# Inverse softmax sums of a banded attention: one turn for two head pairs and a way through DRAM in place of six turns, and K loaded for four heads

## The chip, the cores and the metric

The kernel runs on one core of one Trainium2 chip. The core has a matrix engine (PE, with a separate path PEld that loads stationary operands), a vector engine (DVE), an activation engine (ACT), a general engine (POOL) and a queue (SP) that issues transfers between DRAM and on-chip memory, which 16 DMA engines carry. Each engine works through its own queue in order. The metric is the device time of one execution in microseconds; the figure for the kernel before is the median of 3 runs.

## The reference

Two stages. The first is an attention of 4 batches, 8 heads, 768 positions and head size 64, in which a query sees the 96 latest keys and the first 8 (global) keys; the second sends each of the 3072 resulting rows of 512 through a mixture of 8 experts whose weights are balanced by eight rounds of row and column normalisation.

```python
scores = scale * np.matmul(q, k.transpose(0, 1, 3, 2)) + bias   # bias: distance times a slope per head
scores = np.where(keep, scores, -1000000000.0)
a = np.exp(scores - np.max(scores, axis=-1, keepdims=True))
a = a / (np.sum(a, axis=-1, keepdims=True) + 1e-09)
x = np.matmul(a, v)                     # then (B*S, H*D)
P = balanced(np.exp(x @ w_gate))        # 8 rounds over rows and columns
out = sum(P[:, e:e+1] * (np.maximum(x @ w1[e], 0.0) @ w2[e]) for e in range(E))
```

The change lies in the division by the sums (fourth line) and in the loading of k.

## The kernel before

The attention takes the first 320 us or so, and the experts the rest. While the attention runs, part of the first expert's work (`filler`, tiles `h_ps` and `y_ps`) is woven between its steps, so that PE always has something to do.

**Items, groups and iterations.** The attention is cut into 32 items `n`: batch, half of the sequence (384 queries) and pair of heads `g`. An item has three groups, one per tile of 128 queries, which gives 96 groups `t`, with `n = t // 3`. `unit(u)` covers one half of one batch, that is four items and twelve groups; its loop takes two groups in each iteration, so six groups, two items, make three iterations, and the position in them is `t % 6` = 0, 2 or 4. This text calls the two items a pair; there are 16 pairs.

**One iteration**, in the order of the program, which PE keeps strictly (class `InOrder`): `ahead` computes the scores `s_ps` of the groups four later and their softmax numerators; `flush` multiplies the numerators of the last iteration by V into `o_ps`; `turn` transposes the numerators of this iteration (`t_ps`, copied to `pT`); `between` is called three times and issues filler products and, through `work`, spills and one `combine` on POOL; at the end stands either `prepare(n + 3)`, for `t % 6` = 0 and 4, or `invert(n)` and `invert(n + 1)`, for `t % 6` = 2.

**Sums.** `softmax` (L293) takes a maximum on DVE (L309), an exponential on ACT that also accumulates the sum (L313) into `sm`, and for the last group of an item adds epsilon on ACT (L316), takes the reciprocal on DVE (L317) and spreads the six columns to 128x384 on ACT (L319, tile `inv`). `invert` (L408) turns this with three products on PE (`r_ps`) and copies the result back on DVE (L414). When an item's last group has been flushed, DVE multiplies `o_ps` by `inv` (L404), ACT rounds to `xh` (L405) and DVE takes the remainder `xl` (L406).

**Loads.** `prepare(n)` transposes q and k of an item (tile `tp`), splits them into two parts on ACT (L266) and DVE (L267) and ends with `load_qk(n + 2)`: two transfers for q (L232) and five or seven for k of two heads (L218). `load_v` brings v for four heads at once. `turned` gives the PSUM bank for these turns, from a ring of two banks that `t_ps`, `tp`, `r_ps` and the gate's turn share (within unit 0, all of these but `t_ps` take theirs from the fillers' ring of two). `combo` writes to a ring `xout` of three buffers, from which spills go to DRAM (L817).

PE's order is that of the program. On the other engines and on SP the framework chooses the order when the program is built: among what its own model of time holds ready, it takes what comes first in the program (`schedule_with_timeline_sim=True`, L1086). A transfer that depends on an earlier one waits on SP before it is issued.

Of the kernel before, what the change touches and what calls it, by code (L numbers as in the profile page):

```python
# [8 lines left out]
F32 = mybir.dt.float32  # L9
# [6 lines left out]
DRAM = bass.MemoryType.DRAM  # L16

P = 128
# [5 lines left out]
UT = 3  # L24
# [8 lines left out]
CHUNK = 2  # L33
LAG = 6
FG = 2
GROUPS = (((0, 0), (1, 0)), ((0, 1), (1, 1)), ((0, 2), (1, 2)))
# [78 lines left out]
class Banded:  # L115
# [5 lines left out]

    SLOTS = 8 * len(GROUPS)
    QK, V = UT + 4, 5
    RAW = QK * P + V * 2 * P
    BIAS1 = 4 * P

    SCRATCH = RAW + 3 * P

    def __init__(self, tc, q, k, v, early, n_bias):

        self.tc, self.nc = tc, tc.nc
        self.q, self.k, self.v = q, k, v
        self.H, self.D = q.shape[1], q.shape[3]
        assert n_bias == self.H * self.BIAS1
        self.bias1, rest = early, early[:, n_bias:]
        self.early_raw = rest[:, 0:self.RAW]
        self.d1 = early[:, n_bias - self.BIAS1:n_bias]
        self.d0 = rest[:, self.RAW:self.RAW + P]  # L140
        self.warm = rest[:, self.RAW + P:].bitcast(mybir.dt.bfloat16)
        self.work = [(b, half, g) for b in range(q.shape[0]) for half in range(2) for g in range(self.H // 2)]
        self.pending = []
        self.sums, self.inv, self.outs = {}, {}, {}
        self.pe = InOrder(tc)
        self.qk, self.vs, self.ready, self.scored = {}, {}, {}, {}

    def open(self, ctx, ident, idle):

        tc = self.tc  # L150
        self.ident, self.idle = ident, idle
        self.raw = ctx.enter_context(tc.tile_pool(name="f_raw", bufs=1, side="right"))
        self.bias0 = self.raw.tile([P, self.H, P], F32, name="bias0")
        self.opd = ctx.enter_context(tc.tile_pool(name="f_opd", bufs=2, side="right"))
        self.wrk = ctx.enter_context(tc.tile_pool(name="f_wrk", bufs=AHEAD + CHUNK, side="right"))
        self.ps = ctx.enter_context(tc.tile_pool(name="f_ps", bufs=2, space=PSUM))

    def distances(self, ng, nl):

# [57 lines left out]
            slot -= shift if slot > 1 + half else 0  # L217
            self.nc.sync.dma_start(out=dst[p:p + w, slot].rearrange("p (j d) -> p j d", j=heads), in_=src[row:row + w, tile])  # L218

    def load_qk(self, n):  # L220
        if n >= len(self.work):
            return
        b, half, g = self.work[n]
        if n % 2 == 0:
            t = self.early_raw[:, 0:self.QK * P]
        else:
            t = self.raw.tile([P, self.QK * P], F32, name="raw_qk")
        t = t.rearrange("p (t c) -> p t c", c=P)
        q_r, k_r = t[:, 0:UT], t[:, UT:]
        for j in range(2):  # L230
            src = self.q[b, 2 * g + j].rearrange("(t p) d -> p t d", p=P)
            self.nc.sync.dma_start(out=q_r[:, :, j * self.D:(j + 1) * self.D], in_=src[:, half * UT:(half + 1) * UT])  # L232
        self.load_heads(k_r, self.k, n, 2, [x for x in PIECES[half] if x[0] != 2 + half], 1)
        self.qk[n] = q_r, k_r

    def load_v(self, n):

        if n >= len(self.work):
            return
        if n % 4 == 0:  # L240
            t = self.early_raw[:, self.QK * P:]
        else:
            t = self.raw.tile([P, self.V * 2 * P], F32, name="raw_v")
# [8 lines left out]
    def prepare(self, n):  # L252

        if n >= len(self.work):
            return
        nc = self.nc
        self.ready[n] = tuple(self.opd.tile([P, w], F32R, name=name)
                              for name, w in (("qh", UT * P), ("ql", UT * P), ("kh", 4 * P + P // 2), ("kl", 4 * P + P // 2)))
        q_r, k_r = self.qk[n]
        qh, ql, kh, kl = self.ready[n]  # L260
        for src, hi, lo, nb in ((q_r, qh, ql, UT), (k_r, kh, kl, UT + self.work[n][1])):
            tp = self.turned("tp")
            for t in range(nb):
                self.pe.transpose(out=tp[:, t], in_=src[:, t], identity=self.ident)
            tp = tp.rearrange("p t c -> p (t c)")[:, 0:nb * P]
            nc.scalar.copy(out=hi[:, 0:nb * P], in_=tp)  # L266
            nc.vector.tensor_tensor(out=lo[:, 0:nb * P], in0=tp, in1=hi[:, 0:nb * P], op=ALU.subtract)  # L267
        self.load_qk(n + 2)

    def scores(self, ts):  # L270

# [21 lines left out]
    def softmax(self, t, s_list):  # L293


        nc, D = self.nc, self.D
        n, group = divmod(t, len(GROUPS))
        _, half, g = self.work[n]
        p_sb = self.wrk.tile([P, 2, 2, P], F32, name="p_sb")
        mx = self.wrk.tile([P, 2], F32, name="mx", bufs=4)  # L300
        if group == 0:
            self.sums[n] = self.wrk.tile([P, UT, 2], F32, name="sm", bufs=4)
        sm = self.sums[n]
        views = []
        for u, (j, i) in enumerate(GROUPS[group]):
            h = 2 * g + j
# [4 lines left out]
        for u, pv in enumerate(views):  # L311
            j, i = GROUPS[group][u]
            nc.scalar.activation(out=pv, in_=pv, func=AF.Exp, bias=mx[:, u:u + 1], scale=-1.0,  # L313
                                 accum_out=sm[:, i, j:j + 1])
        if group == len(GROUPS) - 1:
            nc.scalar.add(sm, sm, EPS)  # L316
            nc.vector.reciprocal(out=sm, in_=sm)  # L317
            self.inv[n] = self.wrk.tile([P, UT, P], F32, name="inv", bufs=3)
            nc.scalar.copy(out=self.inv[n].rearrange("p t (j d) -> p (t j) d", j=2),  # L319
                           in_=sm.rearrange("p t j -> p (t j)").unsqueeze(2).broadcast_to([P, 2 * UT, D]))  # L320
        return p_sb

    def blocks(self, n, group):
# [29 lines left out]
    def unit(self, u, xh, xl, between):  # L353
# [2 lines left out]

        NG, per = len(GROUPS), len(GROUPS) * (self.H // 2)
        if u == 0:
            self.load_qk(1)
            self.prepare(0)  # L360
            self.scale_bias(0)
            self.keep_warm(self.ps, "o", WARM0)
# [8 lines left out]
        for t in range(u * per, (u + 1) * per, CHUNK):  # L371
            self.ahead(range(t + AHEAD, t + AHEAD + CHUNK))
            self.flush()
            for t1 in range(t, t + CHUNK):
# [2 lines left out]
                    self.outs[n] = self.ps.tile([P, UT, P], F32, name="o_ps", tag="o", bufs=2)  # L377
                g = n % (self.H // 2)
                self.pending.append((n, group, self.turn(t1), self.outs[n], xh[g], xl[g]))
            for c in (CHUNK, 1, 1):  # L380
                between(c)
            n = t // NG
            if t % (2 * NG) == CHUNK:
                self.invert(n)
                self.invert(n + 1)
            else:
                self.prepare(n + NG)
        self.idle = None

# [15 lines left out]
        self.nc.scalar.copy(out=xh, in_=o_ps)  # L405
# [368 lines left out]
def pipeline(tc, attention, ident, moe, acc, scratch):  # L774
# [12 lines left out]
    with ExitStack() as top:  # L787
# [230 lines left out]
def kernel(  # L1018
# [72 lines left out]
```

## Time and profile before

| | us |
|---|---|
| median of 3 runs (2199.28 to 2199.98) | 2199.44 |
| the profiled execution | 2199.65 |
| its span, first to last instruction | 2197.9 |
| PE busy in the span | 2177.2 |
| DVE busy | 1329.1 |
| POOL busy | 1127.9 |
| ACT busy | 757.1 |

The span lies within the execution; about 1.8 us of it are outside. The profile's rows name a group by line, engine, operation and tiles (`out<-in`), with the count, the busy time and the mean of one, and then the idle time of the engine just before them with what ended it. Most matrix instructions stand under L109 and transposes under L112, the helper's lines, and are told apart by their tiles. Since products overlap in PE, the duration of one is longer than the room that it takes; the chain of waits, which follows the work back from the last instruction, shows the room.

### The profile page before, as it was taken

What the parts mean: (1) busy time and instruction counts of PE and PEld (TensorE: products, weight loads), DVE (VectorE), ACT (ScalarE), POOL (GpSimd) and SP (SyncE); (2) the same over time, 40 slices, a digit from 0 to 9 for tenths busy, and PEclk for the clock granted to TensorE, in tenths of its full rate; (3) what the DMA queues carried; (4) which work ended last, traced back from release to release, by engine and by line L of the source; (5) the groups of instructions that cost most, each with busy time, mean ns of one, the idle gap of its engine ahead of it and who ended that gap; (6) DMA issues with size and microseconds to landing.
All of it is one profiled execution on the core that took longest, in us unless ns stands there. A gap on an engine that the chain in (4) does not pass through costs nothing.

```text
span 2197.9 us, 29372 instructions
## 1 busy us (share of the span) xinstructions
PE 2177.2 (99%) x10851; PEld 1811.4 (82%) x10851; DVE 1329.1 (60%) x2348; ACT 757.1 (34%) x1540; POOL 1127.9 (51%) x1061
## 2 busy tenths in 40 slices
PE   7999999999999999999999999999999999999998
PEld 5888888888888888888888888888888888888887
DVE  6555546756656666665665665665566566566565
ACT  6677763322222222223232222222232223222231
POOL 5767565445445445445455554544454545545440
PEclk8999999999999999999999999999999999999999
DMA  5666553111111111171111111111611111111111
GB/s 122 162 194 175 144 165 128 48 58 48 49 58 48 55 51 48 58 259 50 57 48 58 48 49 58 49 51 55 201 57 49 49 58 49 58 48 49 58 39 50
DMA packets 207817, 173.47 MB, mean 79 GB/s; under 512 B 102704, under 2 KB 170800, under 8 KB 207664
## 3 DMA queue, kind: packets, MB, share of 16 engines
q1 hardware_dynamic: 207664, 171.51, 25.3%
q8 instruction: 87, 1.43, 0.3%
q14 instruction: 66, 0.54, 0.1%
HBM read 142.36 MB, written 29.10 MB: 78 GB/s over the span
## 4 chain that ended last, share of the span: by engine, by line
PE 97%; ACT 1%; DVE 1%; DMA 0%; SPq 0%; issue 0%; POOL 0%; ACTq 0%; DVEq 0%
PE y_ps L109 46%; PE bank_a L109 11%; PE bank_d L109 11%; PE bank_c L109 11%; PE bank_b L109 5%; PE h_ps L109 3%; PE o_ps L109 2%; PE s_ps L109 2%; PE t_ps L112 2%; PE tp L112 1%; PE r_ps L112 1%; PE g_ps L109 0%; ACT p_sb L313 0%; PE y_ps L705 0%; PE y_ps L704 0%; PE y_ps L703 0%
## 5 line engine op out<-in xcount | busy, mean ns | idle before, releaser
L990 DVE SCALAR_TENSOR_TENSOR early<-y_ps,pm,early 128x512 f32<-128x512 f32 x672 | 503.0, 749 | 241.8 <-PE y_ps L109 241.3
L563 POOL TENSOR_TENSOR wl<-wsum,wh 128x1280 fp32r<-128x1280 f32 x90 | 266.2, 2957 | 577.8 <-ACT wh L562 577.8
L585 POOL TENSOR_TENSOR wsum<-w1f 128x256 f32<-128x256 f32 x450 | 317.5, 740 | 319.1 <-DMA w1f<-in_moe_w_dram 319.1
L109 PE MATMUL y_ps<-w2h,h_set 128*128 128x512 f32 x1408 | 433.5, 389 | 0.0
L109 PE MATMUL y_ps<-w2h,x 128*128 128x512 f32 x1408 | 433.4, 389 | 0.0
L562 ACT CAST w2h<-w2f 128x1024 fp32r<-128x1024 f32 x90 | 94.8, 1054 | 688.6 <-issue 610.6
L109 PEld LDWEIGHTS y_ps<-w2h,h_set 128*128 128x128 f32 x1408 | 264.3, 188 | 54.9
L109 PEld LDWEIGHTS y_ps<-w2h,x 128*128 128x128 f32 x1408 | 264.3, 188 | 54.9
L109 PE MATMUL y_ps<-w2l,h_set 128*128 128x512 f32 x704 | 274.1, 389 | 0.1
L109 PE MATMUL y_ps<-w2l,x 128*128 128x512 f32 x704 | 273.9, 389 | 0.0
L109 PE MATMUL bank_a<-m,wh 128*128 128x512 f32 x696 | 242.8, 389 | 1.0 <-DVE h_set L635 1.0
L109 PE MATMUL bank_d<-x,wh 128*128 128x512 f32 x696 | 242.7, 389 | 0.0
L109 PE MATMUL bank_c<-x,wh 128*128 128x512 f32 x696 | 242.5, 389 | 0.0
L563 POOL TENSOR_TENSOR w2l<-w2f,w2h 128x1024 fp32r<-128x1024 f32 x90 | 216.0, 2400 | 48.5 <-ACT w2h L562 48.5
L675 DVE TENSOR_TENSOR early<-early,bank_d 128x512 f32<-128x512 f32 x90 | 62.0, 689 | 175.8 <-PE bank_d L109 171.8
L109 PEld LDWEIGHTS y_ps<-w2l,h_set 128*128 128x128 f32 x704 | 132.1, 188 | 27.8 <-DVE early L990 0.5
L109 PEld LDWEIGHTS y_ps<-w2l,x 128*128 128x128 f32 x704 | 132.1, 188 | 27.5
L109 PEld LDWEIGHTS bank_a<-m,wh 128*128 128x128 f32 x696 | 130.6, 188 | 29.0 <-DVE h_set L635 1.9
L109 PEld LDWEIGHTS bank_c<-x,wh 128*128 128x128 f32 x696 | 130.6, 188 | 27.1
L109 PEld LDWEIGHTS bank_d<-x,wh 128*128 128x128 f32 x696 | 130.6, 188 | 27.1
L109 PE MATMUL bank_a<-m,wl 128*128 128x512 f32 x348 | 135.4, 389 | 0.0
L109 PE MATMUL bank_d<-x,wl 128*128 128x512 f32 x348 | 135.4, 389 | 0.0
(233 smaller groups left out, 3480.8 us busy)
## 6 DMA issues: line engine op xcount, KB each, us to landing
w1f<-in_moe_w_dram SPq DMA_DIRECT2D x92, 512.0 KB, 3.5
w2f<-in_moe_w_dram SPq DMA_DIRECT2D x92, 512.0 KB, 3.4
x<-op_m SPq DMA_DIRECT2D x16, 512.0 KB, 7.6
op_m<-op SPq DMA_DIRECT2D x30, 256.0 KB, 2.8
m<-op_m SPq DMA_DIRECT2D x12, 512.0 KB, 7.2
out_dram<-early SPq DMA_DIRECT2D x24, 256.0 KB, 4.0
ys<-y_sb SPq DMA_DIRECT2D x21, 256.0 KB, 2.8
early<-ys SPq DMA_DIRECT2D x21, 256.0 KB, 4.1
```

What stands on the lines that cost most here:

```text
L109: return self.tc.keep_in_program_order(self.engine.matmul(*args, **kw))
L112: return self.tc.keep_in_program_order(self.engine.transpose(*args, **kw))
L562: self.nc.scalar.copy(out=hi, in_=full)
L563: self.nc.gpsimd.tensor_tensor(out=lo, in0=full, in1=hi, op=ALU.subtract)
L585: nc.gpsimd.tensor_tensor(out=s[:, n], in0=x, in1=y, op=op)
L675: tt(out=t3, in0=t3, in1=d, op=ALU.subtract)
L990: nc.vector.scalar_tensor_tensor(out=a, in0=y_ps, scalar=moe.pm[:, tt, e:e + 1], in1=a, op0=ALU.mult, op1=ALU.add)
```

## The change

1. Sums of a pair of items are kept in one tile `[P, 2, 2, 3]` (head, item, tile of queries). The spreading on ACT and the three turns per item on PE go, with the copy on DVE.
2. `turn_sums`, at the end of the iteration `t % 6` = 0 and ahead of `prepare`, turns the twelve columns of a pair with one product into 12 rows of 128, copies them with ACT and writes them to DRAM.
3. `load_sums`, in the iteration `t % 6` = 2 behind the first `between`, reads the rows back, each head's 768 numbers to the 64 partitions of that head, into one tile `inv` with a single buffer.
4. `load_qk` is split. `load_q` is as before. `load_k` brings k for four heads, two items, with as many transfers as before for two, and is called from `prepare(n)` for odd `n`, for items `n + 3` and `n + 4`.
5. To make room, `xout` goes from three buffers to two, and a few fixed tiles are cut anew.

```diff
     def open(self, ctx, ident, idle):
+        self.dram = ctx.enter_context(tc.tile_pool(name="f_inv", bufs=4, space=DRAM))
-    def load_qk(self, n):
+    def load_q(self, n):
         b, half, g = self.work[n]
+        t = self.early_q if n % 2 == 0 else self.raw.tile([P, self.Q], F32, name="raw_q")
         t = t.rearrange("p (t c) -> p t c", c=P)
         for j in range(2):
             src = self.q[b, 2 * g + j].rearrange("(t p) d -> p t d", p=P)
+            self.nc.sync.dma_start(out=t[:, :, j * self.D:(j + 1) * self.D], in_=src[:, half * UT:(half + 1) * UT])
-        self.load_heads(k_r, self.k, n, 2, [x for x in PIECES[half] if x[0] != 2 + half], 1)
+    def load_k(self, n):
+        half = self.work[n][1]
+        t = self.early_k if n % 4 == 0 else self.raw.tile([P, self.K], F32, name="raw_k")
+        t = t.rearrange("p (t c) -> p t c", c=2 * P)
+        self.load_heads(t, self.k, n, 4, [x for x in PIECES[half] if x[0] != 2 + half], 1)
+        self.ks[n], self.ks[n + 1] = t[:, :, 0:P], t[:, :, P:]
...
     def prepare(self, n):
-        self.load_qk(n + 2)
+        self.load_q(n + 2)
+        if n % 2:
+            self.load_k(n + 3)
     def softmax(self, t, s_list):
-        if group == 0:
-            self.sums[n] = self.wrk.tile([P, UT, 2], F32, name="sm", bufs=4)
-        sm = self.sums[n]
+        if t % (2 * len(GROUPS)) == 0:
+            self.sums[n] = self.sums[n + 1] = self.wrk.tile([P, 2, 2, UT], F32, name="sm", bufs=2)
+        sm = self.sums[n][:, :, n % 2]
...
         if group == len(GROUPS) - 1:
             nc.scalar.add(sm, sm, EPS)
             nc.vector.reciprocal(out=sm, in_=sm)
-            self.inv[n] = self.wrk.tile([P, UT, P], F32, name="inv", bufs=3)
-            nc.scalar.copy(out=self.inv[n].rearrange("p t (j d) -> p (t j) d", j=2),
-                           in_=sm.rearrange("p t j -> p (t j)").unsqueeze(2).broadcast_to([P, 2 * UT, D]))
     def unit(self, u, xh, xl, between):
         if u == 0:
-            self.load_qk(1)
+            self.load_q(1)
+            self.load_k(2)
...
-            for c in (CHUNK, 1, 1):
-                between(c)
             n = t // NG
+            between(CHUNK)
             if t % (2 * NG) == CHUNK:
-                self.invert(n)
-                self.invert(n + 1)
-            else:
+                self.load_sums(n)
+            between(1)
+            between(1)
+            if t % (2 * NG) == 0:
+                self.turn_sums(n)
+            if t % (2 * NG) != CHUNK:
                 self.prepare(n + NG)
-    def invert(self, n):
-        inv = self.inv[n]
-        r_ps = self.turned("r_ps")
-        for i in range(UT):
-            self.pe.transpose(out=r_ps[:, i], in_=inv[:, i], identity=self.ident)
-        self.nc.vector.tensor_copy(inv, r_ps[:, 0:UT])
+    def turn_sums(self, n):
+        rows = 4 * UT
+        tp = self.turned("r_ps")
+        self.pe.transpose(out=tp[0:rows, 0], in_=self.sums.pop(n).rearrange("p j n t -> p (j n t)"), identity=self.ident)
+        del self.sums[n + 1]
+        r_sb = self.wrk.tile([rows, P], F32, name="rows", bufs=1)
+        self.nc.scalar.copy(out=r_sb, in_=tp[0:rows, 0])
+        self.spread[n] = self.dram.tile([rows, P], F32, name="rows_d")
+        self.nc.sync.dma_start(out=self.spread[n], in_=r_sb)
+    def load_sums(self, n):
+        inv = self.wrk.tile([P, 2, UT, P], F32, name="inv", bufs=1)
+        src = self.spread.pop(n).rearrange("(j m) p -> j (m p)", j=2)
+        self.nc.sync.dma_start(out=inv.rearrange("p n t c -> p (n t c)"),
+                               in_=src.unsqueeze(1).broadcast_to([2, self.D, 2 * UT * P]))
+        self.inv[n], self.inv[n + 1] = inv[:, 0], inv[:, 1]
...
-        xout = att.enter_context(tc.tile_pool(name="xout", bufs=3))
+        xout = att.enter_context(tc.tile_pool(name="xout", bufs=2))
...
-    band.load_qk(0)
+    band.load_q(0)
+    band.load_k(0)
     band.load_v(0)
```

More of the change, by code (lines that the diff above doesn't have):

```diff
@@ L124 @@
     SLOTS = 8 * len(GROUPS)
-    QK, V = UT + 4, 5
-    RAW = QK * P + V * 2 * P
+    Q, K, V = UT * P, 4 * 2 * P, 5 * 2 * P
     BIAS1 = 4 * P
-    SCRATCH = RAW + 3 * P
+    SCRATCH = Q + K + V + P
     def __init__(self, tc, q, k, v, early, n_bias):
@@ L137, in __init__ @@
         self.bias1, rest = early, early[:, n_bias:]
-        self.early_raw = rest[:, 0:self.RAW]
+        self.early_q = rest[:, 0:self.Q]
+        self.early_k = rest[:, self.Q:self.Q + self.K]
+        self.early_v = rest[:, self.Q + self.K:self.Q + self.K + self.V]
+        self.d0 = rest[:, self.Q + self.K + self.V:]
         self.d1 = early[:, n_bias - self.BIAS1:n_bias]
-        self.d0 = rest[:, self.RAW:self.RAW + P]
-        self.warm = rest[:, self.RAW + P:].bitcast(mybir.dt.bfloat16)
+        warm = n_bias - 2 * self.BIAS1
+        self.warm = early[:, warm:warm + 2 * P].bitcast(mybir.dt.bfloat16)
         self.work = [(b, half, g) for b in range(q.shape[0]) for half in range(2) for g in range(self.H // 2)]
         self.pending = []
-        self.sums, self.inv, self.outs = {}, {}, {}
+        self.sums, self.spread, self.inv, self.outs = {}, {}, {}, {}
         self.pe = InOrder(tc)
-        self.qk, self.vs, self.ready, self.scored = {}, {}, {}, {}
+        self.qs, self.ks, self.vs, self.ready, self.scored = {}, {}, {}, {}, {}
     def open(self, ctx, ident, idle):
@@ L223, in load_qk @@
         b, half, g = self.work[n]
-        if n % 2 == 0:
-            t = self.early_raw[:, 0:self.QK * P]
-        else:
-            t = self.raw.tile([P, self.QK * P], F32, name="raw_qk")
+        t = self.early_q if n % 2 == 0 else self.raw.tile([P, self.Q], F32, name="raw_q")
         t = t.rearrange("p (t c) -> p t c", c=P)
-        q_r, k_r = t[:, 0:UT], t[:, UT:]
         for j in range(2):
             src = self.q[b, 2 * g + j].rearrange("(t p) d -> p t d", p=P)
-            self.nc.sync.dma_start(out=q_r[:, :, j * self.D:(j + 1) * self.D], in_=src[:, half * UT:(half + 1) * UT])
-        self.load_heads(k_r, self.k, n, 2, [x for x in PIECES[half] if x[0] != 2 + half], 1)
-        self.qk[n] = q_r, k_r
+            self.nc.sync.dma_start(out=t[:, :, j * self.D:(j + 1) * self.D], in_=src[:, half * UT:(half + 1) * UT])
+        self.qs[n] = t
+    def load_k(self, n):
+        if n >= len(self.work):
+            return
+        half = self.work[n][1]
[3 more added lines that the diff above has]
+        self.ks[n], self.ks[n + 1] = t[:, :, 0:P], t[:, :, P:]
     def load_v(self, n):
@@ L239, in load_v @@
             return
[L240 to L243, printed above, removed]
+        t = self.early_v if n % 4 == 0 else self.raw.tile([P, self.V], F32, name="raw_v")
         t = t.rearrange("p (t c) -> p t c", c=2 * P)
@@ L258, in prepare @@
                               for name, w in (("qh", UT * P), ("ql", UT * P), ("kh", 4 * P + P // 2), ("kl", 4 * P + P // 2)))
-        q_r, k_r = self.qk[n]
+        q_r, k_r = self.qs[n], self.ks[n]
         qh, ql, kh, kl = self.ready[n]
@@ L313, in softmax @@
             nc.scalar.activation(out=pv, in_=pv, func=AF.Exp, bias=mx[:, u:u + 1], scale=-1.0,
-                                 accum_out=sm[:, i, j:j + 1])
+                                 accum_out=sm[:, j, i:i + 1])
         if group == len(GROUPS) - 1:
@@ L379, in unit @@
                 self.pending.append((n, group, self.turn(t1), self.outs[n], xh[g], xl[g]))
-            for c in (CHUNK, 1, 1):
-                between(c)
             n = t // NG
+            between(CHUNK)
             if t % (2 * NG) == CHUNK:
-                self.invert(n)
-                self.invert(n + 1)
-            else:
+                self.load_sums(n)
[4 more added lines that the diff above has]
+            if t % (2 * NG) != CHUNK:
                 self.prepare(n + NG)
```

## The prediction

> **What bounds the kernel now.** I read the page first, then the busy time by stages.
>
> ```profile
> span 2197.9 us, 29372 instructions
> PE 2177.2 (99%) x10851; PEld 1811.4 (82%) x10851; DVE 1329.1 (60%) x2348; ACT 757.1 (34%) x1540; POOL 1127.9 (51%) x1061
> ...
> 0.00:20.00 20.00, 13.12 (x62) 8.07 (x64) 11.84 (x47) 6.37 (x20) 16.39 (x36) 0.79 0.45 99
> 20.00:55.00 35.00, 29.49 (x279) 24.07 (x276) 25.27 (x92) 27.29 (x95) 11.78 (x12) 0.87 0.57 135
> 55.00:100.00 45.00, 43.87 (x376) 38.37 (x372) 22.77 (x88) 31.67 (x100) 33.27 (x39) 1.00 0.64 169
> 100.00:300.00 200.00, 200.00 (x1713) 174.93 (x1711) 109.44 (x397) 141.07 (x441) 139.30 (x159) 1.00 0.61 166
> ```
>
> A stage row gives length, busy time of PE, PEld, DVE, ACT and POOL, granted clock, DMA share and GB/s. From 100 us on PE is never idle, so a product less is time saved and a wait of PE is time lost, one for one. Before that PE idles 6.9 + 5.5 + 1.1 = 13.5 us. DVE, at 109 of 200 us, has room.
>
> **What goes on PE.** The chain of waits shows the room that turns take; the first block is from a pair in the steady part, the second has the turns of the first three pairs.
>
> ```profile
> 191.81 0.77 PE tp L112 x7
> ...
> 198.59 0.66 PE r_ps L112 x6
> ...
> 204.75 0.77 PE tp L112 x7
> ...
> 207.45 1.02 PE t_ps L112 x8
> ```
> ```profile
> 30.52 1.28 PE r_ps L112 x6
> ...
> 44.19 0.55 PE r_ps L112 x3
> ...
> 58.57 0.65 PE r_ps L112 x6
> ```
>
> Six turns of sums take 0.66 us, 0.11 each, in each of the 13 pairs after the start: 8.6 us. The three pairs of the start give 1.28 + 0.55 + 0.65 = 2.5. Out go 11.1 us; 16 turns of twelve columns at 0.11 (an estimate by the same 128 moving columns) come in, 1.8. The net is **-9.3 us**. ACT's spreading and DVE's copies also go; from 100 us on that is worth nothing by itself, as both have room (141 and 109 of 200 us busy), and at the start it is counted with the waits below.
>
> **What the moved turn waits for.** PE keeps the program's order, so the new turn, at the place where the first `tp` stands, waits for the reciprocal of the later item; `prepare` and the next scores queue behind it.
>
> ```profile
> 191.14 0.22 ACT L316 ACTIVATE sm<-sm 128x6 f32<-128x6 f32 x1
> 191.65 0.93 PE L112 MATMUL tp<-ident,raw_qk 128*128 128x128 f32 x7
> 191.84 0.18 DVE L317 RECIPROCAL sm<-sm 128x6 f32<-128x6 f32 x1
> ...
> 131.87 1.15 PE L112 MATMUL tp<-ident,raw_qk 128*128 128x128 f32 x7
> 132.10 0.19 DVE L317 RECIPROCAL sm<-sm 128x6 f32<-128x6 f32 x1
> ...
> 172.10 0.82 PE L112 MATMUL tp<-ident,raw_qk 128*128 128x128 f32 x6
> 172.11 0.18 DVE L317 RECIPROCAL sm<-sm 128x6 f32<-128x6 f32 x1
> ...
> 151.86 0.19 DVE L317 RECIPROCAL sm<-sm 128x6 f32<-128x6 f32 x1
> 152.62 0.82 PE L112 MATMUL tp<-ident,raw_qk 128*128 128x128 f32 x6
> ...
> 38.00 0.49 PE L112 MATMUL tp<-ident,raw_qk 128*128 128x128 f32 x3
> 42.84 0.18 DVE L317 RECIPROCAL sm<-sm 128x6 f32<-128x6 f32 x1
> ...
> 52.44 1.24 PE L112 MATMUL tp<-ident,raw_qk 128*128 128x128 f32 x7 [1.26 <-ACT pT L336]
> 54.70 0.18 DVE L317 RECIPROCAL sm<-sm 128x6 f32<-128x6 f32 x1
> ...
> L112 PE MATMUL r_ps<-ident,inv 128*128 128x128 f32 x96 | 14.0, 282 | 1.5 <-ACT inv L319 1.5
> L112 PEld LDWEIGHTS r_ps<-ident,inv 128*128 128x128 f32 x96 | 12.0, 146 | 2.9 <-ACT inv L319 1.7
> ...
> 38.53 0.34 ACT L336 COPY pT<-t_ps 128x256 f32<-128x256 f32 x1
> ```
>
> The reciprocal ends 0.37, 0.42 and 0.19 us after `tp` starts in the first three, and early in the fourth; these four kinds alternate. With 0.18 for the signal and the loading of weights (an estimate: one load lasts 0.146) that is 0.55, 0.60, 0.37 and 0, three pairs of each and one early pair more: **+4.6 us**. Above nothing the bound is open only if the framework places L316 or L317 elsewhere; placed earlier, the term is 0.
>
> The turn also takes one of two banks, so that the second half of `tp` waits for ACT's small copy: 0.28 for the product, 0.28 for the copy and 0.08 for two signals (estimates; 128x256 takes 0.34), against 0.44 of cover by the turn and the first half: +0.2 a pair, between 0 and 0.5, **+2.7**. In the start ACT is what PE waits for, and the reciprocals end 5.0 and 2.4 us after their `tp` start (43.02 and 54.88, against 38.00 and 52.44). Their epsilon could run earlier; about half of the 7.4, 4.0, is taken, between 0 and 8.
>
> **K.** Late K stops PE at two places.
>
> ```profile
> 23.57 1.91 DMA raw_qk<-in_k_dram
> ...
> 93.20 0.33 PE L112 MATMUL tp<-ident,raw_qk 128*128 128x128 f32 x1 [1.13 <-DMA raw_qk<-in_k_dram]
> ...
> 197.84 3.12 SPq L218 DMA_DIRECT2D raw_qk<-in_k_dram  x6
> ...
> L609 POOL TENSOR_TENSOR op<-xsum,xres 128x256 fp32r<-128x256 f32 (+1 forms) x40 | 35.0, 874 | 11.2 <-DMA op_m<-op 8.4
> ```
>
> An issue holds SP some 0.5 us (3.12 for six). K for four heads saves half of 192 issues, the rows' way adds 32, and K comes one to two items earlier: the 1.1 us at 93 go, and at the start 0.8 (what late is next there is the moved turn). **-1.9**. `xout` with two buffers costs nothing where a spill lands within the next `combine`, five operations of 0.874, 4.4 us. In before POOL waited 8.4 us for spills in all; twice that would still be POOL's time, which has 61 of 200 us to spare, and reaches PE only through SP.
>
> Without the read-back, then, -9.3 + 4.6 + 2.7 + 4.0 - 1.9 = **+0.1 us**.
>
> **The read-back.** It moves 2 x 64 x 3072 bytes, 393 KB, issued on SP behind the small write, two transfers of q and five to seven of K. The trace has no transfer like it: its source has two rows, each read 64 times.
>
> ```profile
> op_m<-op SPq DMA_DIRECT2D x30, 256.0 KB, 2.8
> ...
> raw_qk<-in_k_dram SPq DMA_DIRECT2D x40, 16.0 KB, 1.9
> ...
> w1f<-in_moe_w_dram SPq DMA_DIRECT2D x4, 512.0 KB, 4.6
> ...
> 1500.00:1520.00 20.00, 20.00 (x90) 16.57 (x89) 12.16 (x19) 5.71 (x9) 9.85 (x10) 1.00 0.17 53
> ...
> 201.58 0.56 DVE L404 TENSOR_TENSOR o_ps<-o_ps,inv 128x384 f32<-128x384 f32 x1
> ...
> 203.60 0.48 ACT L405 CAST x<-o_ps 128x384 fp32r<-128x384 f32 x1
> ...
> 205.72 0.56 DVE L267 TENSOR_TENSOR ql<-tp,qh 128x384 fp32r<-128x384 f32 x1 [0.95 <-ACT qh L266]
> ```
>
> Spread over 16 engines it lands 4 us after issue (between 2.8 for 256 KB and 4.6 for 512). If it is divided by its outermost count, two engines carry 196.6 KB each. A busy engine moves 166 / (16 x 0.61) = 17 GB/s at 100 to 300 us, where pieces are mostly 256 bytes, and 53 / (16 x 0.17) = 19.5 with the weights' 1 to 2 KB; for 3 KB I take 22, an estimate along that row. That is 8.9 us plus the 1.9 of the smallest transfer: 10.8. In the diff the outermost dimension is two heads, while every loaded row of before counts 32 or more partitions outermost, so no row is near in what matters. I take two engines, and keep both ends.
>
> From the turn, T: copy 0.75, write 0.5, q 1.0, K 2.7, so the read is issued at T + 4.9 (the write has landed by then, 1.9 after its issue) and lands at T + 15.7. The multiply stood at 201.58, 9.8 after the `tp` at 191.81, and comes at T + 9.3 as 0.66 of PE's work ahead of it goes and part returns. DVE then stands **6.4 us** in its queue, once a pair. Behind it are `xl`, the splits of `prepare` and the next maxima; on ACT the rounding (L405), and behind that the copies of `tp`. The rounding stood 1.46 us behind the end of the multiply, and the first half of `tp` was split at 206.28, 1.2 us ahead of `t_ps`, which needs the bank; some 0.5 comes from the spreading that ACT no longer does. PE is covered for 3.1 us and loses 3.3 a pair: 43 in 13 pairs, and 2 in each of the first three, where it idles already. **+49 us**, between 24 (landing 2 us sooner, if SP is ahead) and 80. The two engines would also be busy 0.61 x 20.0 + 8.9 = 21.1 us in a pair's 20.0 (seven pairs from 58.57 to 198.59), so what else they carry comes later too, which points to the upper half.
>
> The Trainium skill ("DMA: Bandwidth & Descriptors", section "Why a DMA increments its semaphore by 16 and not by 1") says that a transfer issued by SP uses the largest number of engines up to 16 that divides the outermost count of both sides; its "Rules for kernel authors" name a repeated source with a small outermost count. That would be two here, and the sum +49. No run here shows it yet. By the row of w1f alone it would be +0.
>
> **Rivals.** (a) *Two engines, hidden.* DVE's order puts other work ahead of the multiply, or SP the read ahead of K; only the crowding of two engines is left, 0 to 15 us: about 2206. For it: `o_ps` has two buffers, two iterations of slack. Against it: ACT's rounding waits for the multiply and stands ahead of the copies that free `tp`'s bank. (b) *Spread, and the moved turn eats the gain*: landing at T + 8.9 is before the multiply, and +0.1 is left, 2199.6. (c) *The other side, faster*: spread, and PE does not wait. Its place is the end of the iteration `t % 6` = 0, its price the 4.6 + 4.0 of waits; it decides as soon as the reciprocal ends before `tp`'s old start. Then 2199.4 - 8.5 = 2191.
>
> **How the numbers follow.** Forecast 2199.4 + 0.1 + 49 = **2248 us**, chance 0.58 (its own range 2218 to 2280); (a) 0.12, (b) 0.16, (c) 0.14. The sum is made in the profiled execution (2199.65, span 2197.9); the median is 0.2 lower and is the base. A measurement of this kernel tells about 0.2%, 4.4 us, from no change. Slower by more: 0.58 and most of (a), 0.68; within: most of (b) and the rest of (a), 0.18; faster: (c), 0.14. The range takes in the forecast's range, (a) and (b): 2194 to 2280.
>
> **What would show it.** Right: in the attention `inv` lands some 10 us after its issue, DVE's longest waits are L404's on it, about 6 us a pair, PE idles 3 us ahead of `t_ps`, and 100 to 300 us holds fewer products. The moved turn is right if PE waits up to 0.6 us for L317 ahead of it. Wrong: `inv` lands in 4 us, or L404 waits and PE does not; then (a) to (c) decide by PE's wait ahead of the twelve-column turn.

## The result, and the profile after

| | before | after |
|---|---|---|
| median | 2199.44 us | **2320.38 us** (5 runs, 2317.21 to 2323.53) |
| ratio after to before, with its 95% interval | | 1.0549 [1.0537, 1.0561] |
| span of the profiled execution | 2197.9 us | 2316.7 us |

The changed kernel is slower by 121 us; the prediction was 2248, with 2280 as its upper end. The sign was right, the size was not. (One of the nine runs of x2_k_only, below, was slow, 3655.76 us at a granted clock of 0.556; ratios are of the fast runs.) The first view is the page of after, its engines and the granted clock in 40 slices; the second is its busy time by stages, with the columns shown for before.

```profile
PE 2204.6 (95%) x10771; PEld 1825.4 (79%) x10771; DVE 1316.5 (57%) x2316; ACT 751.5 (32%) x1524; POOL 1127.3 (49%) x1061
...
PEclk7888989899999999999999999999999999999999
```
```profile
20.00:55.00 35.00, 18.15 (x138) 14.38 (x136) 13.49 (x51) 14.94 (x55) 18.10 (x16) 0.65 0.61 149
55.00:100.00 45.00, 31.11 (x255) 25.82 (x254) 18.70 (x70) 22.09 (x71) 17.77 (x26) 0.78 0.44 115
100.00:300.00 200.00, 163.61 (x1257) 138.72 (x1256) 74.87 (x279) 105.56 (x332) 93.86 (x93) 0.90 0.50 143
```

From 100 to 300 us PE runs 1257 products where before ran 1713, is busy for 163.61 us instead of 200, and at a clock of 0.90 instead of 1.00. All the loss is in the attention: the first product of the experts that follow it (`x_ps`) starts at 447.24 us instead of 328.12, 119 us later, and what comes after takes as long as before. The next view has busy time from 20 us to that product, for before and then for after.

```profile
20.00:328.12 308.12, 301.49 (x2568) 261.82 (x2565) 167.60 (x604) 216.74 (x677) 196.93 (x223) 0.99 0.60 163
```
```profile
20.00:447.24 427.24, 328.54 (x2486) 276.21 (x2483) 155.54 (x572) 211.54 (x661) 198.07 (x225) 0.86 0.47 132
```

PE's idle time went from 6.6 us (308.12 - 301.49) to 98.7, and its busy time from 301.5 to 328.5 with fewer products, as some run at half clock.

The chain of waits of after, up to 460 us, names the read-back; 15 of the 16 pairs are on it. From 20 to 447 us the landing of `inv` has 37.6% of the chain, and no spill is on it. Shown are the first two pairs, and one pair of the steady part with a piece of what follows on PE.

```profile
34.14 12.32 DMA inv<-rows_d
...
57.86 12.02 DMA inv<-rows_d
...
216.50 9.83 DMA inv<-rows_d
...
230.62 1.70 PE o_ps L109 x16
```

The timeline of the same pair, engine by engine (PE, SP, DVE, ACT; start, duration, work, and in brackets the idle time ahead and what ended it):

```profile
209.26 0.27 PE L112 MATMUL r_ps<-ident,sm 128*12 128x128 f32 x1
...
228.14 0.90 PE L112 MATMUL tp<-ident,raw_k 128*128 128x128 f32 x3 [5.07 <-ACT pT L342]
...
212.50 0.47 SPq L427 DMA_DIRECT2D rows_d<-rows  x1
...
213.49 2.95 SPq L223 DMA_DIRECT2D early<-in_k_dram  x6
216.50 0.54 SPq L434 DMA_DIRECT2D inv<-rows_d  x1
...
226.42 0.57 DVE L414 TENSOR_TENSOR o_ps<-o_ps,inv 128x384 f32<-128x384 f32 x1 [7.26 <-DMA inv<-rows_d]
...
227.03 0.48 ACT L415 CAST x<-o_ps 128x384 fp32r<-128x384 f32 x1 [6.26 <-DVE o_ps L414]
227.51 0.58 ACT L342 COPY pT<-t_ps 128x512 f32<-128x512 f32 x1
...
228.60 0.34 SPq L885 DMA_DIRECT2D ys<-y_sb  x1
```

This is the mechanism that was forecast: the turn at 209.26 (T), the read issued behind K at T + 7.2, landed 9.8 us later; DVE stands 7.3 us for it, ACT's rounding stands behind the multiply, and a copy of `pT` behind the rounding, so that the second half of `tp` gets its bank late. Seen so, the read's landing explains the case. PE's own rows among the waits of after, summed from 20 to 460 us (total, times, longest), say the same. But POOL has a row that is not on this path (its wait for `op_m`), and the list of DMA issues (count, KB each, median us to landing) one that shows why:

```profile
DVE o_ps L414 <- DMA inv<-rows_d: 122.3, 15, 13.6
...
POOL op L631 <- DMA op_m<-op: 63.4, 9, 12.3
...
PE tp L112 <- ACT pT L342: 44.6, 8, 6.9
...
PE o_ps L109 <- DVE pT L342: 19.5, 2, 11.9
...
PE o_ps L109 <- ACT pT L342: 11.1, 2, 6.5
...
PE t_ps L112 <- DVE ql L274: 10.0, 3, 4.4
...
PE r_ps L112 <- DVE sm L326: 7.9, 4, 2.6
```
```profile
op_m<-x SPq DMA_DIRECT2D x16, 128.0 KB, 10.0
```

In before POOL waited 8.4 us for its spills in all, and the 128 KB spills landed in 2.3 us. PE's rows sum to 93.1 of its 98.7 us of idle time: 85.2 for copies of `pT` and for a split of q that stand behind the late multiply, and 7.9 for the reciprocal ahead of the moved turn. None of them ends on a spill. The experiments had to tell how much of the 121 us is the late multiply and how much is other transfers that are late.

### The profile page after: what moved, and what is told of

Read it like the earlier page. It is cut to its first block, busy times and chain, and to the rows that moved or that the text cites. A ratio compares the mean times of both kernels' runs of the same rounds, so it can differ in the third digit from the quotient of the medians.

```text
span 2316.7 us, 29082 instructions
## 1 busy us (share of the span) xinstructions
PE 2204.6 (95%) x10771; PEld 1825.4 (79%) x10771; DVE 1316.5 (57%) x2316; ACT 751.5 (32%) x1524; POOL 1127.3 (49%) x1061
## 4 chain that ended last, share of the span: by engine, by line
PE 88%; DMA 8%; SPq 1%; ACT 1%; DVE 1%; issue 1%; POOL 0%; DVEq 0%; ACTq 0%
PE y_ps L109 43%; PE bank_a L109 10%; PE bank_d L109 10%; PE bank_c L109 10%; DMA inv<-rows_d 7%; PE bank_b L109 5%; PE s_ps L109 1%; PE o_ps L109 1%; PE h_ps L109 1%; PE tp L112 1%; PE t_ps L112 1%; SPq L223 1%; DVE o_ps L414 0%; PE y_ps L726 0%; PE y_ps L727 0%
```

## The experiments

For each kernel one table row is drawn from its timeline: from each turn of sums (`r_ps`, 16 of them) to the next multiply by `inv`, the median over pairs 4 to 16; the mean period of a pair, from the fourth turn to the sixteenth; and the start of the fourth turn, which shows what the start cost. For after, and for the kernel without a read, the fourth and sixteenth turns are these rows:

```profile
103.28 0.27 PE L112 MATMUL r_ps<-ident,sm 128*12 128x128 f32 x1
...
422.38 0.27 PE L112 MATMUL r_ps<-ident,sm 128*12 128x128 f32 x1
```
```profile
76.26 0.27 PE L112 MATMUL r_ps<-ident,sm 128*12 128x128 f32 x1
...
312.05 0.27 PE L112 MATMUL r_ps<-ident,sm 128*12 128x128 f32 x1
```

```
kernel                    time us  ratio [95%]              turn to   period  fourth
                                                            multiply  of pair turn at
after                     2320.38  1.0549 [1.0537, 1.0561]  17.0      26.6    103.3
x1_two_reads              2217.02  1.0083 [1.0066, 1.0099]  11.5      20.3     81.9
x4_turn_late              2224.50  1.0118 [1.0101, 1.0135]  11.7      20.9     84.8
x3_keep_clock             2336.91  1.0630 [1.0613, 1.0648]  18.5      28.2    100.8
x5_four_engines           2283.03  1.0377 [1.0359, 1.0394]  15.8      24.8     94.8
x6_k_behind_read          2288.77  1.0409 [1.0392, 1.0427]  14.5      25.0     92.3
x7_two_reads_k_behind     2210.87  1.0056 [1.0039, 1.0072]   9.8      19.9     80.2
x8_no_read                2200.64  1.0003 [0.9994, 1.0013]   9.6      19.7     76.3
x9_fill_stall             2332.20  1.0603 [1.0585, 1.0620]  16.7      27.7    105.2
x10_read_unused           2274.65  1.0345 [1.0328, 1.0362]   9.9      24.2     79.3
x11_two_unused            2199.46  0.9997 [0.9988, 1.0007]   9.6      19.7     76.3
x12_late_two_reads        2241.43  1.0182 [1.0165, 1.0199]  16.2      22.0     89.3
```

x2_k_only has no such turn: 2193.64 us, 0.9974 [0.9964, 0.9985].

### Two reads in place of one

```diff
-        self.nc.sync.dma_start(out=inv.rearrange("p n t c -> p (n t c)"),
-                               in_=src.unsqueeze(1).broadcast_to([2, self.D, 2 * UT * P]))
+        for j in range(2):
+            self.nc.sync.dma_start(out=inv[j * self.D:(j + 1) * self.D].rearrange("p n t c -> p (n t c)"),
+                                   in_=src[j:j + 1].broadcast_to([self.D, 2 * UT * P]))
```

> The changed kernel, but the rows are read back by two transfers, one for each head, each with 64 partitions outermost on both sides, in place of one with two heads outermost. The same bytes, the same repeated rows, one issue more. Theory (few engines): the read-back lands about 10 us after its issue because its outermost count is 2 and two engines carry it. Then here it lands in 3 to 5 us, DVE's multiply waits under 1 us a pair, the clock stays at 1.0 after the start, and the time is 2192 to 2206 us. Rival (repeated rows): reading one row of DRAM 64 times is what is slow; then the landing stays near 10 us and the time above 2290. Rival (the rest of the change): K, the smaller ring of combine buffers or the moved turn cost the 120 us; then the time stays above 2290 though the read lands early.

The same bytes as two transfers, each with 64 partitions outermost, bring 2217.02 us: 103 of the 121 us go. The DMA issues of this kernel, and its waits for the read from 20 to 350 us:

```profile
inv<-rows_d SPq DMA_DIRECT2D x32, 192.0 KB, 3.6
```
```profile
DVE o_ps L414 <- DMA inv<-rows_d: 29.4, 13, 4.5
```

Each row is still read 64 times, so a repeated source is not what was slow. The trace's records of single packets say the same: the 128 pieces of 3072 bytes take 121 ns each in the median in both kernels, and a pair's 128 pass in 8.1 to 9.9 us in after and in 1.9 to 3.9 here. Sixty-four pieces in a row, half of them, take 64 x 0.121 = 7.7 us, which fits two engines.

### K for four heads alone

```diff
-    band.load_qk(0)
+    band.load_q(0)
+    band.load_k(0)
...
-        xout = att.enter_context(tc.tile_pool(name="xout", bufs=3))
+        xout = att.enter_context(tc.tile_pool(name="xout", bufs=2))
```

The kernel before with `load_q`, `load_k` and the two buffers of the change; the sums are spread and turned as in before.

> The kernel before with K for four heads at once and the ring of two combine buffers (three don't fit beside the larger K tile), and with the old spreading and the six turns. Theory: K comes earlier, the wait of 1.1 us at 93 and part of the start go: 2196 to 2200 us. Rival (the smaller ring or the larger K transfers hold up POOL and SP): above 2204 us, with POOL's waits on spills well over the 8.4 us of before.

2193.64 us, 5.9 faster than before on that chip (2199.58): a little under the expected range, and the one version that is faster than both kernels. Its stages show where:

```profile
20.00:55.00 35.00, 30.53 (x319) 25.47 (x317) 27.20 (x102) 30.52 (x106) 20.46 (x21) 0.98 0.82 197
55.00:100.00 45.00, 45.00 (x390) 39.63 (x387) 24.10 (x93) 31.72 (x102) 32.88 (x37) 1.00 0.64 178
```

The 1.1 us of idle PE behind 55 us are gone, as forecast; at 20 to 55 us PE is busy for 1.0 us more, and its clock is 0.98 instead of 0.87, which the forecast did not count.

### The turn behind `prepare`

```diff
-            if t % (2 * NG) == 0:
-                self.turn_sums(n)
             if t % (2 * NG) != CHUNK:
                 self.prepare(n + NG)
+            if t % (2 * NG) == 0:
+                self.turn_sums(n)
```

(On the kernel with two reads.)

> As the run with two reads, and the twelve-column turn stands behind prepare's transposes, not ahead of them. Theory (the moved turn waits for the reciprocal and for a bank): PE's waits of up to 0.6 us ahead of it and the 0.3 us between the halves of tp go, 13 pairs of about 0.5 us, so it is 5 to 9 us faster than the run with two reads, at 2186 to 2199 us. Rival (those waits are covered): within 2 us of the run with two reads. Rival (rows come too late): the turn is 0.8 us later, the multiply waits, and it is slower.

2224.50 us, 7.5 slower than with the turn in its place. PE's wait for the reciprocal is smaller (6.8 us for 10.7), but the turn now waits for the split of q on DVE that frees its bank, and the waits for the read are no shorter (33.3 for 29.4). The waits from 20 to 350 us:

```profile
DVE o_ps L414 <- DMA inv<-rows_d: 33.3, 10, 7.1
...
PE r_ps L112 <- DVE ql L274: 10.5, 12, 1.0
...
PE r_ps L112 <- DVE sm L326: 6.8, 3, 3.6
```

One wait took the place of the other.

### Four engines

```diff
-        self.spread[n] = self.dram.tile([rows, P], F32, name="rows_d")
-        self.nc.sync.dma_start(out=self.spread[n], in_=r_sb)
+        self.spread[n] = self.dram.tile([2, 2, rows // 2, P], F32, name="rows_d")
+        for c in range(2):
+            for j in range(2):
+                self.nc.sync.dma_start(out=self.spread[n][j, c], in_=r_sb[6 * j:6 * j + 6])
...
-                               in_=src.unsqueeze(1).broadcast_to([2, self.D, 2 * UT * P]))
+                               in_=src.unsqueeze(1).broadcast_to([4, self.D // 2, 2 * UT * P]))
```

> The changed kernel with the twelve rows written to DRAM twice (four small writes in place of one), so that the read-back's outermost count is four in place of two. If the outermost count sets the number of engines, four carry 98 KB each, the read lands 5 to 6.5 us after its issue (two engines 10 to 12; two separate reads 3.6), and the time stands between those two kernels: 2235 to 2270, nearer to the upper end if the three more writes hold SP up. If a repeated source is slow as such, however it is counted, the landing stays near 10 and the time is 2320 or a little more.

2283.03 us, between the other two, but above the expected range, and so is the landing: by the chain of waits from 100 us on it takes 6.8 to 8.5 us, where 5 to 6.5 was expected.

```profile
106.00 6.83 DMA inv<-rows_d
...
228.85 8.52 DMA inv<-rows_d
```

A pair's 128 pieces pass in 4.9 to 6.6 us by the packet records, against 32 x 0.121 = 3.9 for four engines that do nothing else. So landings and packets agree in all three kernels with an outermost count that sets the number of engines. The time fell by less than the landing because the read is also issued later, 7.7 us behind the turn in the median instead of 6.2, as three more writes stand ahead of it on SP; the multiply comes only 1.2 us sooner (15.8 for 17.0). Spills are on this kernel's chain too, `op_m<-op` with 4.3% of it from 100 to 430 us against 26.2% for `inv`.

### K issued behind the read

```diff
-        if n % 2:
+        if n % 2 and n < len(GROUPS):
             self.load_k(n + 3)
...
                 self.load_sums(n)
+                self.load_k(n + 2 * NG)
```

Once on the changed kernel, once on the one with two reads.

> The changed kernel with its one read over two engines, but K for four heads is issued behind the read-back instead of ahead of it. The trace showed the read issued 7.2 us after the turn, some 3 us of it behind K's six transfers, where the prediction had 4.9. If the issue's delay is a term of the loss as the landing is, the read comes 3 us sooner in nearly all pairs, DVE's wait on it falls from a mean of 8 us to 5, and the time falls by 3 x 15 = 45 plus some of the half clock: 2255 to 2280. If the landing alone decides, or later K stops PE as much, 2310 to 2330.

> Two reads, one per head, which landed in 3.6 us, and K issued behind them. If the 17.5 us that two reads left over the kernel before come from the read's late issue, it now lands near the time at which the multiply is due, DVE's waits on it in the attention fall from 29 to under 10 us in all, and the time is 2198 to 2207. If they come from the moved turn's wait for the reciprocal and from the start, it stays at 2213 to 2220.

With one read, 2288.77 us: the multiply comes 2.5 us sooner (14.5 for 17.0 behind the turn) and 31.6 us go, less than expected. With two reads, 2210.87: the multiply comes 9.8 us behind the turn, as early as it can (9.6 below), DVE's waits for the read fall from 29.4 to 13.7 us, and still only 6 of the 17.5 us go, less than expected. Of the 10.2 us that are left over the kernel without a read, 3.9 lie in the start (the fourth turn is at 80.2 us) and 3.1 in the twelve periods behind it.

### No read at all

```diff
-        inv = self.wrk.tile([P, 2, UT, P], F32, name="inv", bufs=1)
-        src = self.spread.pop(n).rearrange("(j m) p -> j (m p)", j=2)
-        self.nc.sync.dma_start(...)
+        if n == 0:
+            self.const = self.wrk.tile([P, 2, UT, P], F32, name="inv", bufs=1)
+            self.nc.vector.memset(self.const, 0.01)
+        inv = self.const
```

> The read-back is left out: the numerators are multiplied by a constant instead of the inverse sums (the sums are still formed, inverted, turned and written). This is the forecast's sum without the read-back, +0.1 us, by itself. K for four heads alone gave -5.9, where the forecast had -1.9, so by the forecast's other terms 2191 to 2200. If the moved turn's waits for the reciprocal and the bank cost more than 0.55 and 0.2 a pair, as PE's waits of up to 3.5 us with two reads suggest, 2204 to 2214. Under 2190 would mean that the moved turn costs nothing.

2200.64 us; the forecast's sum without the read-back was 2199.5. The multiply comes 9.6 us after the turn when it waits for nothing (forecast: 9.3). In the steady part the gate's product `g_ps`, once in two pairs, gives the gain of the turns against the moved turn's waits; first before, then this kernel, four of its periods:

```profile
137.20 1.05 PE L109 MATMUL g_ps<-x,ghl 128*128 128x384 f32 x5
...
295.33 1.58 PE L109 MATMUL g_ps<-x,ghl 128*128 128x384 f32 x8
```
```profile
140.32 1.57 PE L109 MATMUL g_ps<-x,ghl 128*128 128x384 f32 x8
...
297.95 1.23 PE L109 MATMUL g_ps<-x,ghl 128*128 128x384 f32 x6
```

That is 158.13 / 8 = 19.77 us a pair in before and 157.63 / 8 = 19.70 here: six turns fewer and one more are worth 0.06 us a pair, about 0.8 in all.

### The read kept, the wait taken away

```diff
-        self.inv[n], self.inv[n + 1] = inv[:, 0], inv[:, 1]
+        if n == 0:
+            self.const = self.wrk.tile([P, UT, P], F32, name="const", bufs=1)
+            self.nc.vector.memset(self.const, 0.01)
+        self.inv[n] = self.inv[n + 1] = self.const
```

The first kernel is the changed one, with its read over two engines into a tile that nobody uses; the second has the two reads over all engines instead.

> The changed kernel with its read over two engines, which lands as late as before, but nothing uses it: the numerators are multiplied by a constant, so that the division by the sums is left out. What is left over the kernel without a read (2200.6) is the crowding of two engines and SP's place. The forecast's rival of two engines hidden gave 0 to 15 us for it, 2206. If the wait of the multiply makes the loss, 2200 to 2212. If the crowding of other transfers (spills, the experts' weights, K) is a good part of the 120 us, 2230 or more.

> As the kernel whose read nothing uses (2274.7; a constant stands for the inverse sums), but the read is two transfers, one per head, over all engines. If the 74 us which the unused read cost over the kernel without a read come from two engines being held for some 8 us, they go: 2200 to 2208, and what two used reads cost beyond that (2217.0) is their wait at the multiply. If 393 KB more a pair, or SP's place, cost them, 2230 or more.

These two price the crowding by itself. With nobody waiting for it, the read over two engines still costs 2274.65 - 2200.64 = **74 us**; the same bytes over all engines cost nothing (2199.46). Bytes and the write of the rows are the same in both, and the dearer one has an issue a pair less on SP, so it is the two engines. In the kernel with the unused read over two engines the waits from 20 to 420 us are these, the last two from PE's own list (20 to 400 us):

```profile
POOL op L634 <- DMA op_m<-op: 111.7, 11, 19.4
...
ACT y_sb L887 <- DMA ys<-y_sb: 35.3, 7, 9.3
```
```profile
PE h_ps L109 <- ACT y_sb L887: 30.4, 6, 8.9
...
PE tp L112 <- DMA early<-in_q_dram: 10.4, 2, 8.0
```

Its chain of waits from 100 to 300 us has no `inv` any more. It has the spills of the filler's results (the first two of five), three of which SP issues right behind the read, as here the first:

```profile
109.91 9.93 DMA ys<-y_sb
...
159.25 7.02 DMA ys<-y_sb
```
```profile
109.28 0.54 SPq L434 DMA_DIRECT2D inv<-rows_d  x1
109.91 0.41 SPq L888 DMA_DIRECT2D ys<-y_sb  x1
```

These spills landed in 2.8 us in before (the median of 21). Issued behind the read they take 7 to 11, ACT has no free `y_sb` until then, and PE's next filler product waits for ACT. POOL waits in the same way for its spills, SP for POOL (64.6 us in 18 waits on its `op`), and the loads behind them on SP come late: the small write of the rows stands 13.5 us behind its turn in the median, 1.7 in after.

In after itself this path does not reach PE. There, in the pair shown above, the next spill of `ys` is issued 12.1 us behind the read (228.60 for 216.50), when the read has landed, and neither PE's waits nor the chain from 20 to 447 us have a spill. The 74 us are a second limit: what sets the time once nobody waits for the read.

### The wait kept, the crowding taken away

```diff
-            if t % (2 * NG) == CHUNK:
-                self.load_sums(n)
...
+            if t % (2 * NG) == 2 * CHUNK:
+                self.load_sums(t // (2 * NG) * 2, self.scored[max(self.scored)])
             self.flush()
...
-    def load_sums(self, n):
+    def load_sums(self, n, late):
         inv = self.wrk.tile([P, 2, UT, P], F32, name="inv", bufs=1)
+        self.nc.scalar.copy(out=inv[:, 0, 0, 0:1], in_=late[:, 0, 0, 0:1])
```

(On the kernel with two reads.)

> Two used reads over all engines, held back: a one-column copy on ACT into the tile, from the latest numerators of the iteration of the multiply, must run first. No engine is crowded, but the multiply comes 13.5 to 15.5 us after the turn instead of 9.6 (the two-engine kernel with K behind the read: 14.5 median, 2288.8 us). If the wait of the multiply alone makes the loss at that lateness, 2270 to 2295. If the crowding of two engines makes much of it and the wait is covered in part, as forecast (3.1 us covered, about 2 lost a pair), 2225 to 2250.

2241.43 us, with the multiply 16.2 us behind the turn, nearly as late as in after (17.0). This late multiply, without crowding, costs 41 us over the kernel without a read: 2.4 us a pair in the period, and 13 in the start (the fourth turn at 89.3 for 76.3). Its waits from 20 to 370 us:

```profile
DVE o_ps L414 <- DMA inv<-rows_d: 42.2, 14, 5.4
...
PE r_ps L112 <- DVE sm L326: 30.9, 13, 8.3
```

The stand-in isn't exact: the framework knew of the late copy and put other work ahead of the multiply on DVE, so that DVE waits 3.0 us a pair, where it waits 8.2 in after, and PE waits ahead of the turn as well. So 41 us is not the price of the wait in after. That 41 and the 74 of the crowding come to about the 120 of both (2320.38 - 2200.64) does not show that the two add up in after.

What the wait costs there can be read from its own timeline. A period is the time from a turn to the next multiply, plus the time from there to the next turn; it is also PE's idle time plus its busy time. The means over the twelve periods from the fourth turn to the sixteenth:

```
kernel               turn to   multiply to  period   PE idle  PE busy
                     multiply  next turn    of pair
x8_no_read             9.6       10.1        19.7      0.2      19.5
after                 17.2        9.4        26.6      5.3      21.3
x12_late_two_reads    16.2        5.8        22.0      1.8      20.2
x10_read_unused       12.7       11.5        24.2      3.4      20.8
```

In after the multiply comes 7.7 us later than without a read, and of that only 0.7 us is made up before the next turn. PE idles 5.1 us more, nearly all of it in waits that end on the multiply's path, and takes 1.9 us longer for its products. That is the whole loss of 6.9 us a pair, with nothing left over for the crowding but what it adds to the read's own landing (9.8 to 12.3 us, where 7.7 of pieces and 1.9 of the smallest transfer make 9.6, an estimate). In x12 4.3 us are made up, since DVE does other work during the wait. In x10 a pair takes 24.2 us by the crowding alone, less than the 26.6 that the wait makes of it in after, which fits that the crowding does not show there.

### The half clock

```diff
+    def fill_idle(self, n):
+        w_ps = self.ps.tile([P, 512], F32, name="w_ps", tag="s0", bufs=1)
+        for m in range(n):
+            one = self.ident.bitcast(mybir.dt.bfloat16)
+            self.pe.matmul(w_ps[:, 0:2 * P], lhsT=one[:, 0:P], rhs=one, start=(m == 0), stop=(m == n - 1))
...
+            if t % (2 * NG) == 2 * CHUNK and t < 90:
+                self.fill_idle(40)
             if t % (2 * NG) != CHUNK:
                 self.prepare(n + NG)
```

On the changed kernel; the second try has 30 products between the two halves of that `prepare`.

> The changed kernel, with 40 products of 256 columns into a score bank that is free there, issued ahead of prepare in the iteration in which PE stalls; their result is used by nothing. They take about 4.3 us of the idle time. Theory (clock): PE's idle time of 5 us a pair halves its clock for the next 3 to 10 us, which costs 2 us a pair on top of the wait itself; with the gap filled the clock stays at 1.0 in most pairs and the time falls by 20 to 35 us, to 2285 to 2300. Rival (the wait alone): the half clock falls in idle time and costs nothing; the time stays within 5 us of 2320 or rises.

> The changed kernel with 30 products of 256 columns that nothing reads (3.3 us at full clock), placed inside the stall: between the turns of q and of k in the prepare that follows the late multiply, in 15 of the 16 pairs (not in the first). PE stands there about 5 us and then runs some 7 us at half clock. If the half clock after the stall lengthens the time, as worked out from the busy time (some 36 of the 121 us), most of the half-clock stretches behind 100 us go and the time falls by 15 to 30 us: 2290 to 2305. If the slower products are hidden behind the next pair's read anyway, it stays within 6 us of 2320. If PE's stall is shorter than the filling in many pairs, or the clock falls in spite of it, 2326 or more.

In both the theory of the clock missed, and the time rose, as the last rival of each had allowed: 2336.91 and 2332.20 us, slower than after by 16.5 and 11.8. The clock did rise (a mean of 0.983 and 0.979 for 0.971), and the time rose too. In the first the products stand ahead of the stall, and the read came later (7.8 us behind the turn in the median, 6.2 in after). In the second, PE's timeline shows why filling can't be aimed:

```profile
209.71 0.55 PE L112 MATMUL tp<-ident,early 128*128 128x128 f32 x3 [3.83 <-ACT pT L350]
210.09 5.11 PE L109 MATMUL w_ps<-ident 128*128 128x256 bf16 x30
215.03 0.49 PE L112 MATMUL tp<-ident,early 128*128 128x128 f32 x3
...
235.11 3.44 PE L109 MATMUL w_ps<-ident 128*128 128x256 bf16 x30
239.89 0.55 PE L112 MATMUL tp<-ident,raw_k 128*128 128x128 f32 x3 [1.34 <-ACT pT L350]
```

In one pair the stall was ahead of the first half and the products came behind it, as pure delay, and slowly (5.11 us for the 3.44 of the next); in the next they lay in the stall. What the half clock costs by itself is thus not shown.

## Why the prediction was wrong

**The step that failed** is the price of the wait: "PE is covered for 3.1 us and loses 3.3 a pair: 43 in 13 pairs, and 2 in each of the first three, where it idles already", +49 us. Against the kernel without a read, a pair of after loses 6.9 us (26.6 - 19.7) and each of the first three 9 ((103.3 - 76.3) / 3), which is 13 x 6.9 + 3 x 9 = 117 us. With 117 in its place the sum would have been 2199.4 + 0.1 + 117 = 2316.5. Three parts make up the 68 us between 49 and 117:

- *The cover, about 31.* PE idles 5.1 us for a multiply that is 7.7 late, so 2.6 us are covered, near the 3.1. But its products then take 1.9 us longer a pair, many of them at half clock, and 0.7 is left of the cover. The sum put slower products at nothing and gave no reason. Whether PE would have gained these 1.9 us at full clock is not shown.
- *The start, about 21.* "Where it idles already" did not hold. Without a read PE idles 2.0 us on average in the first three pairs, while the multiply came 10 us later there (18.5 us behind the turn for 8.5), and DVE's copies of `pT`, for which PE waited up to 11.9 us, stood behind it.
- *The lateness, about 16.* The multiply came 7.7 us late instead of 6.4, as the read was issued 1.3 us later than forecast.

PE's place was another, too. The forecast had it idle ahead of `t_ps`; behind 100 us this happened three times, while it stopped eight times at `tp` and twice at `o_ps` for a copy of `pT`.

The crowding was priced wrongly as well, at 0 to 15 us in rival (a), where it is 74 with nobody waiting. The row for it, 21.1 us of work on each of the two engines in a pair's 20.0, was worked out and not followed to the spills that queue there, whose buffers ACT and POOL need again. But it is not what set the time of after, whose chain from 20 to 447 us has no spill.

Its other steps, in their order:

- **PE bound, net of turns and moved turn.** Right in the steady part: -8.6 + 1.4 + 4.6 + 2.7 = +0.1 was forecast over 13 pairs and -0.8 measured.
- **Start waits, +4.0.** Too small. The kernel without a read is 1.2 us above before; with -5.9 for K and -0.8 for the steady pairs, the turns and waits of the start are +7.9, where -2.5 + 0.3 + 4.0 = +1.8 was forecast. PE waited 2.3 to 2.6 us for the reciprocal in each of the first three pairs of after.
- **K, -1.9.** Measured -5.9, with the buffers of `xout`; this error and that of the start nearly cancel.
- **Without the read-back, +0.1.** Measured +1.2 and, with an unused read over all engines, 0.0 us. Right as a sum, by luck, as two of its terms were 4 and 6 us off in opposite directions.
- **The landing, 10.8 us on two engines.** Right: 9.8 to 12.3. The rate estimated at 22 GB/s is 25 by the packets (3072 bytes in 121 ns).
- **Read issued at T + 4.9, multiply due at T + 9.3, DVE stands 6.4.** The read came at T + 6.2 in the median, since SP had other transfers between; the multiply was due at T + 9.6 and came at T + 17.0; DVE stood 122.3 / 15 = 8.2 us.
- **`xout` with two buffers costs nothing where a spill lands within 4.4 us.** The condition failed: spills landed late, POOL waited 63.4 us for them in after, and SP for POOL 70.4 us (19.2 in before), the path that the text had named. It did not reach PE in after. Three buffers were not tried with the read over two engines.
- **The Trainium skill's rule** ("DMA: Bandwidth & Descriptors", section "Why a DMA increments its semaphore by 16 and not by 1"), that the engines used are the largest number up to 16 that divides the outermost count of both sides, agrees with all runs here: counts of 2, 4 and 64 landed in 9.8 to 12.3, 6.8 to 8.5 and 3.6 us.

Of the rivals, (a) was right that the two engines crowd others and wrong that the read would be hidden; (b) and (c) fell with the landing.

## What to carry to other kernels

A transfer that falls on few engines can set the time in two ways: by its own landing, which the consumer's wait shows, and by the landing of everything else that queues on these engines. Here the trace showed the larger of the two, and the other came out when the first was taken away. Where the engines it takes come to more than the loop's period, measure the transfer once with nobody waiting for it before moving its consumer. Here splitting it by the dimension that has many entries took away most of both, 103 of the 121 us. When a wait in a loop is priced, the cover has to be worked out for the start too, and the slower clock behind a stall is a term.

## What the runs showed that was not expected

- An unused transfer of 393 KB a pair cost 74 us on two engines and nothing measurable on all (2274.65 and 2199.46 us). So taking away the wait alone gave back 46 of the 121 us.
- Behind 100 us the granted clock in after fell to a half for 3 to 10 us at a time, behind stalls of PE: after the 5.07 us shown above, sixteen products by V took 1.70 us, where the same sixteen took 1.02 in the kernel without a read. With two reads, where no wait of PE behind 100 us was longer than 1.6 us, it did not fall there.
- A higher granted clock came with a longer time twice (0.983 and 0.979, 2336.91 and 2332.20 us, against 0.971 and 2320.38).
